# Sinkhorn attention and a gated MLP on one core: the first load from ScalarE, another order of loads, column-wise P, wider transposes of V

## The chip, the cores and the metric

The kernel runs on one core of one Trainium2 chip. The metric is the device time of one execution in microseconds. A core has a TensorE for matrix products (PE in the profile, with its weight loads as PEld), a VectorE (DVE), a ScalarE (ACT), a GpSimd (POOL) and a SyncE (SP), each with a queue of its own, and 16 DMA engines that they share.

## The reference, cut to what matters

```python
P = sort_net                                  # [4, 8, 8, 8]
for _ in range(5):
    P = exp(P - max(P, -1))
    P = P / sum(P, -1)                        # rows
    P = P / sum(P, -2)                        # columns
k_sorted = einsum('bhij,bhjcd->bhicd', P, k_b)    # 8 blocks of 96 tokens
v_sorted = einsum('bhij,bhjcd->bhicd', P, v_b)
attn = softmax(q_b @ k_sorted.T / 8)          # inside each block
x = attn @ v_sorted                           # [4, 768, 512] over the heads
h = relu(x @ w_in); u, v = halves of h
v = layer_norm(v)
out = (u * (w_spatial @ v + b_spatial)) @ w_out
```

4 batches, 8 heads, 768 tokens, 64 per head; q, k, v and all weights are fp32 in memory. The kernel works in bf16 with fp32 accumulation.

## The kernel before, in words

The program is a list of short units in the string `ORDER`, written out by hand. The units are run in the order of the string, and each engine's instructions keep that order in its queue. A unit is a name with arguments: `QT:2:D:0:1` is u_QT with the PSUM tile ps2, the copy on VectorE (D; A is ScalarE), batch 0, pair of heads 1. Batches overlap: while one batch is in the gated MLP, the next is in attention.

**Loads.** `S0` loads sort_net into `p_all` from SyncE's queue. `LH:S:0` loads four heads of the first q as fp32 from SyncE; `QC:A:0` and `QC:A:1` cast it to bf16 on ScalarE (L115). All other loads are `L` units (L171 to L188): GpSimd issues them, and the DMA casts fp32 to bf16. In the string they come as v of batch 0, k of batch 0, the rest of q, then batch 1 and the weights. `IV:2` is a memset of a column of ones in `vm` on GpSimd, `ID` makes the identity on GpSimd, `MA`, `MB` and `MC` derive masks from it.

**Start of ScalarE.** Before any unit ScalarE loads its table of exponentials (L125).

**Sinkhorn.** `SK:0` to `SK:4` are the five rounds on a 32 x 64 tile, one row for each batch and head: exponential on ScalarE (L238), then on VectorE the row sums (L239), their reciprocal, the product with it (L243), the column sums (L244), reciprocal, product (L249). The last round ends in `p_t` (L251). `QC:A:0` stands on ScalarE ahead of the fourth exponential, `QC:A:1` ahead of the fifth.

**From P to the sorted blocks.** `PR:1` spreads P over the partitions by eight small products (L256). `P0` units multiply it by a mask on VectorE (L270) into the block matrices `pd` of batch 0, `PC` copies it out for the later batches, whose `PD` units run on GpSimd. `VT` (L383) multiplies the first batch's v with pd and gives it transposed (`vT`); `KT` does so for k. `VB` (L401) turns vT back block by block: eight transposes, each with a weight load of one block of 96 columns and the 128 columns of the identity moving, then one copy into `vb`. The later batches go another way for v (`VM`, and `VC` by DMA from SyncE). On TensorE stand `PR:1`, one QT, `VT:0`, `KT:3`, `VT:2` in this order.

**Attention.** `SC` makes the scores (L442) and their exponential on ScalarE (L447); `AT` the product with vb (L488), the reciprocal (L495) and the scaling (L496) on VectorE. After it come the transposes `XT`, the products `VP`, `UP`, `SP` and `OP` of the MLP, and the weights' transposes `WW` (L531).

**Idle products.** `DM:ps:n:512` are n products of a zero tile on TensorE with 512 columns (L226), which nobody reads. There are 24 before the first QT and 12 between it and `PR:1`.

**Tiles.** The pool `ld` has eight places for loads, a place is given to the next load once all readers of the old one stand earlier in the order. kT tiles go round six places of `kt_all`, whose last 32 columns are zero, so that a weight load of 128 columns at the last block stays inside; vT tiles are a pool tile with two buffers of 768 columns.

Of the kernel before, what the change touches and what calls it, by code (L numbers as in the profile page):

```python
# [8 lines left out]
FP32 = mybir.dt.float32  # L9
BF16 = mybir.dt.bfloat16  # L10
# [3 lines left out]
AX = mybir.AxisListType  # L14
# [1 line left out]


ORDER = """
S0 CO SK:0 BH LH:S:0 IV:2 L:v:0:0:8 SK:1 SK:2 ID MA L:k:0:0:8 L:q:0:4:8 DM:3:6:512 DM:0:6:512 L:v:1:0:8 L:q:1:0:8
QC:A:0 SK:3 QC:A:1 MB SK:4 DM:2:6:512 DM:1:6:512 MC QT:2:D:0:1 DM:1:6:512 DM:3:6:512 PR:1 L:k:1:0:8 QT:2:A:0:0 P0:0:2  # L20
L:wv L:wsb P0:4:6 P0:6:8 IV:0 P0:2:4 PC:D VT:0:A:0:0 KT:3:D:0:0 L:wu PD:1:0:4 VT:2:A:0:1 L:v:2:0:8 KT:1:A:0:3
KT:0:D:0:2 SC:2:0:0:1 VB:3:D:0:0 PD:1:4:8 KT:1:A:0:1 QT:0:D:0:2 IV:1 QT:2:A:0:3 VB:3:D:0:1 SC:0:0:1:0 VT:1:D:0:3
VT:2:A:0:2 L:wsa L:q:2:0:8 SC:3:0:0:0 PD:3:0:4 PD:3:4:8 BI AT:0:0:0:1 L:k:2:0:8 VB:1:D:0:3 SC:2:0:1:1 AT:3:0:0:0
# [42 lines left out]
def kernel(  # L66
# [25 lines left out]
    HP = H // 2  # L92
# [5 lines left out]
    const = ctx.enter_context(tc.tile_pool(name="const", bufs=1))  # L98
# [6 lines left out]
    def ps_tile(n, dt=FP32):  # L105
        return psum.tile([128, 2, 512 if dt == FP32 else 1024], dt, name=f"ps{n}", tag=f"ps{n}")

    def queue(eng):
        if "general" in st:
            return nc.gpsimd  # L110
        return nc.scalar if eng == "A" else nc.sync
# [10 lines left out]
        else:  # L122
            nc.vector.tensor_scalar_max(out=out, in0=in_, scalar1=0.0)

    nc.scalar.preload_act_table_set("natural_log_exp_and_others")  # L125

    p_all = const.tile([BH, NB, NB], FP32, name="p_all")
    p16 = const.tile([BH, NB * NB], BF16, name="p16")
    p_t = const.tile([BH, NB * NB], BF16, name="p_t")
    spread = const.tile([BH, BH, TB], BF16, name="spread")  # L130
# [20 lines left out]
    NE, NK, NZ, NX = 5, 6, 3, 4  # L151
    ex_all = const.tile([BLK, NE, 2 * NI * BLK + 32], BF16, name="ex_all")
    kt_all = const.tile([128, NK, S + 32], BF16, name="kt_all")
    ex = [ex_all[:, n] for n in range(NE)]
    kt = [kt_all[:, n] for n in range(NK)]

    st = {}
    count = {"e": 0, "k": 0}

    def ld_tile(name):  # L160
        return ld.tile([128, H, G * D], BF16, name=name, tag="ld")
# [31 lines left out]
    def u_S0():  # L193
        load_sort_net()

    def u_BI():
        nc.gpsimd.dma_start(
            out=b_bc, in_=_raw_ap(moe_b_spatial, 0, [[0, 128], [1, S]]))

    def u_CO():  # L200
        nc.vector.memset(warm, 0.0)  # L201
        nc.vector.memset(eps_tile, 1e-6)
        nc.vector.memset(ones, 1.0)
        nc.vector.memset(ex_all[:, :, 2 * NI * BLK:], 0.0)
        nc.vector.memset(kt_all[:, :, S:], 0.0)

    def u_ID():
        make_identity(nc, ident)
# [21 lines left out]
    def u_SK(n, safe=False):  # L230
        n = int(n)
        rows, cols = (first[:, 0:NB], first[:, NB:2 * NB]) if n == 0 else (rowsum, colsum)
        over_rows = lambda x: x.to_broadcast([BH, NB, NB])
        over_cols = lambda x: _raw_ap(x, 0, [x.ap[0], [0, NB], x.ap[1]])
        if safe:
            nc.vector.reduce_max(out=rowsum, in_=p_all, axis=AX.X)
            nc.vector.tensor_sub(out=p_all, in0=p_all, in1=over_rows(rowsum))
        nc.scalar.activation(out=p_all, in_=p_all, func=AF.Exp)  # L238
        nc.vector.reduce_sum(out=rows, in_=p_all, axis=AX.X)  # L239
# [3 lines left out]
        nc.vector.tensor_mul(out=p_all, in0=p_all, in1=over_rows(rowsum))  # L243
        nc.vector.reduce_sum(out=cols, in_=p_all.rearrange("p i j -> p j i"), axis=AX.X)  # L244
# [4 lines left out]
        nc.vector.tensor_mul(out=to, in0=p_all, in1=over_cols(colsum))  # L249
        if n == 4:  # L250
            nc.vector.transpose(out=p_t, in_=p16)  # L251

# [142 lines left out]

    def u_VB(ps, eng, b, hp):
        b, hp = int(b), int(hp)
        t = ps_tile(ps, BF16)[0:BLK, 0, :].rearrange("p (i c) -> p i c", i=NB)
        vT = turned("vT", b, hp)
        for i in range(NB):  # L400
            nc.tensor.transpose(t[:, i, :], vT[:, i * BLK:(i + 1) * BLK], ident)  # L401
        copy(
            eng, vb[b % 2][:, :, 2 * hp:2 * hp + 2, 0:D], t.rearrange("p i (h d) -> p i h d", h=2),
        )

    def u_VM(ps, eng, b, hp):
# [10 lines left out]
            t[:, :, 0:G * D].rearrange("p h (g d) -> p h g d", g=G),  # L417
        )

    def u_VC(b, lo, hi):  # L420
        b = int(b)
        for i in range(int(lo), int(hi)):
            queue("S").dma_start(
                out=vb[b % 2][:, i].rearrange("c h d -> c (h d)"),
                in_=vm[i * TB:(i + 1) * TB].rearrange("t g h d -> t g (h d)"),
            )

    def e_tile(b, hp, ih):
# [398 lines left out]
```

## Time and profile before

| | us |
|---|---|
| median of 3 runs | 156.18 (155.99 to 156.47) |
| span of the profiled execution | 154.5 |
| TensorE busy | 146.7 |
| VectorE busy | 115.4 |
| ScalarE busy | 85.5 |
| GpSimd busy | 39.4 |
| first k: from issue to landing | 11.0 |

The span runs from the first to the last instruction of one execution; the run's own time is longer by what lies around it. Busy times count the idle products as work. In a timeline each row has the start, the length, the engine, the line and operation, the tile written and those read, and in brackets how long the engine sat idle before it and what ended that. Rows named SPq and ACTq are issues of DMAs on those queues. In the rows of the DMA queues stand packets, megabytes and the share of 16 engines' time; q0 is the queue that GpSimd's loads use, q1 that of SyncE and ScalarE.

### The profile page before, as it was taken

To read this page: it belongs to the slowest core of one execution; us is meant where nothing else is said; L and a number is where in the kernel's file an instruction comes from. 1 tells how busy PE (TensorE), PEld (TensorE's weight loads), DVE (VectorE), ACT (ScalarE), POOL (GpSimd) and SP (SyncE) were. 2 spreads that over 40 slices of the span, in tenths; PEclk is the share of its full clock that TensorE was granted. 3 is DMA by queue.
4 is the path that set the end of the run, shared out by engine and by line. 5 is a ranking of instruction groups with operands and counts; after the bars stand their busy time and mean duration, and the time that the engine had idled before them with its cause. 6 is when DMAs were issued, how large, how long until landed. Compare 5 with 4: busy or idle time off the path is not lost.

```text
span 154.5 us, 4033 instructions
## 1 busy us (share of the span) xinstructions
PE 146.7 (95%) x1689; PEld 95.7 (62%) x1689; DVE 115.4 (75%) x258; ACT 85.5 (55%) x116; POOL 39.4 (25%) x45
## 2 busy tenths in 40 slices
PE   6988988999999999999999999999999999999991
PEld 2436866764667777456777654656876556774760
DVE  3787889968899976299974886697977629855742
ACT  3345989787979245997777057357650072260040
POOL 7953663292020007000000044000000406103630
PEclk9999999999999999999999999999999999999999
DMA  2999999999999999990069358704708400307756
GB/s 68 270 204 203 204 206 204 209 216 248 223 205 256 205 231 245 208 195 15 4 118 125 67 102 167 182 3 37 205 0 215 163 0 4 132 4 284 268 191 220
DMA packets 30693, 24.36 MB, mean 158 GB/s; under 512 B 10384, under 2 KB 27792, under 8 KB 30672
## 3 DMA queue, kind: packets, MB, share of 16 engines
q0 software_dynamic: 14432, 12.19, 48.8%
q1 hardware_dynamic: 15664, 11.23, 28.8%
q10 hardware_dynamic: 576, 0.66, 1.2%
q8 instruction: 14, 0.23, 0.6%
q14 instruction: 7, 0.06, 0.1%
HBM read 24.78 MB, written 6.29 MB: 201 GB/s over the span
## 4 chain that ended last, share of the span: by engine, by line
PE 84%; DMA 7%; ACT 2%; DVE 2%; POOL 1%; issue 1%; POOLq 0%; ACTq 0%
PE ps L609 15%; PE ps L554 14%; PE ps L597 14%; PE ps L635 10%; DMA k_in<-in_k_dram 7%; PE ps L442 5%; PE ps L488 5%; PE ps L665 5%; PE ps L383 4%; PE ps L685 3%; PE ps L314 2%; PE ps L410 2%; PE ps L518 2%; ACT ex_all L447 2%; PE ps L531 1%; PE ps L401 1%
## 5 line engine op out<-in xcount | busy, mean ns | idle before, releaser
L626 POOL TENSOR_TENSOR gt<-z,u_sb 128x768 bf16<-128x768 f32 x7 | 11.4, 1640 | 77.0 <-DVE z L615 47.6
L447 ACT ACTIVATE ex_all<-ps 96x768 bf16<-96x768 f32 x32 | 24.7, 806 | 5.7 <-PE ps L442 5.5
L609 PE MATMUL ps<-wspT,v_sb 128*128 128x384 bf16 x144 | 25.1, 326 | 0.0
L597 PE MATMUL ps<-xT,w_in_sb 128*128 128x384 bf16 x128 | 22.8, 326 | 0.0
L496 DVE TENSOR_TENSOR x_sb<-ps,rec_all 96x512 bf16<-96x512 f32 x32 | 22.0, 686 | 1.1
L554 PE MATMUL ps<-w_in_sb,xT 128*128 128x512 bf16 x96 | 22.3, 380 | 0.0
L571 DVE BATCH_NORM_STATS2 stats<-v_sb 128x6 f32<-128x512 bf16 x24 | 16.3, 678 | 4.5 <-ACT v_sb L121 4.5
L115 ACT COPY o_sb<-ps 128x1024 f32<-128x1024 f32 (+1 forms) x12 | 10.9, 905 | 14.6 <-PE ps L685 9.1
L609 PEld LDWEIGHTS <-v_sb 128*128 128x128 bf16 x144 | 13.6, 97 | 8.6
L121 ACT ACTIVATE v_sb<-ps 128x1024 bf16<-128x1024 f32 (+1 forms) x11 | 10.3, 948 | 12.3 <-PE ps L554 12.3
L615 DVE TENSOR_TENSOR z<-ps,b_bc 128x768 f32<-128x768 f32 x12 | 11.4, 954 | 7.3 <-PE ps L609 4.6
L635 PE MATMUL ps<-w_out_sb,gt 128*128 128x256 bf16 x144 | 16.9, 273 | 0.0
L121 ACT ACTIVATE u_sb<-ps 128x768 bf16<-128x768 f32 x12 | 9.7, 811 | 12.7 <-PE ps L597 12.7
L597 PEld LDWEIGHTS <-w_in_sb 128*128 128x128 bf16 x128 | 11.8, 97 | 7.2
L635 PEld LDWEIGHTS <-gt 128*128 128x128 bf16 x144 | 13.8, 97 | 2.1
L554 PEld LDWEIGHTS <-xT 128*128 128x128 bf16 x96 | 8.7, 97 | 9.9
L488 PEld LDWEIGHTS <-ex_all 96*128 96x128 bf16 x256 | 10.7, 97 | 4.0 <-issue 0.5
L488 PE MATMUL ps<-vb,ex_all 96*128 96x65 bf16 x256 | 12.6, 193 | 0.5 <-ACT ex_all L447 0.5
L226 PE MATMUL ps<-warm 128*128 128x512 bf16 x36 | 9.5, 425 | 1.3 <-DVE warm L201 1.3
L442 PE MATMUL ps<-qT,kt_all 64*128 64x96 bf16 x256 | 9.8, 205 | 0.9 <-issue 0.4
L115 ACT CAST kt_all<-ps 128x768 bf16<-128x768 f32 x11 | 8.7, 801 | 2.2 <-PE ps L383 2.2
L442 PEld LDWEIGHTS <-kt_all 64*128 64x128 bf16 x256 | 6.4, 94 | 5.5 <-issue 3.3
(97 smaller groups left out, 202.6 us busy)
## 6 DMA issues: line engine op xcount, KB each, us to landing
out_dram<-o_sb SPq DMA_DIRECT2D x9, 512.0 KB, 4.6
v_in<-in_v_dram POOLq DMA_DIRECT2D x4, 768.0 KB, 21.4
k_in<-in_k_dram POOLq DMA_DIRECT2D x4, 768.0 KB, 23.7
vb<-vm SPq DMA_DIRECT2D x24, 99.0 KB, 5.8
q_in<-in_q_dram POOLq DMA_DIRECT2D x3, 768.0 KB, 28.2
ws_in<-in_moe_w_spatial_dram POOLq DMA_DIRECT2D x2, 576.0 KB, 26.6
w_in_sb<-in_moe_w_in_dram POOLq DMA_DIRECT2D x2, 512.0 KB, 24.9
q<-in_q_dram SPq DMA_DIRECT2D x1, 768.0 KB, 4.6
```

The lines of the kernel that those rows point to most:

```text
L115: nc.scalar.copy(out=out, in_=in_)
L121: nc.scalar.activation(out=out, in_=in_, func=AF.Relu)
L442: nc.tensor.matmul(t[:, hh, 0:HW].rearrange("p (g x) -> p g x", g=G)[:, :, ii * TB:(ii + 1) * TB], lhsT=kT[rows, i * BLK:i * BLK + 128], r ...
L447: nc.scalar.activation(out=e_tile(b, hp, ih).rearrange("p h (x g) -> p h x g", g=G), in_=t[0:BLK, :, 0:HW].rearrange("p h (g x) -> p h x g ...
L488: nc.tensor.matmul(t[:, hh, ii * VW:ii * VW + D + 1], lhsT=e[:, c:c + 128], rhs=vb[b % 2][:, ih * NI + ii, 2 * hp + hh, 0:D + 1], start=Tr ...
L496: nc.vector.tensor_mul(out=x_sb[:, hp].rearrange("p i (h d) -> p h i d", h=2), in0=tv[:, :, :, 0:D], in1=_raw_ap(rec, 0, [rec.ap[0], [NI, ...
L554: nc.tensor.matmul(t[:, x, :], lhsT=st["xT", b][:, n // 3, kc, (n % 3) * 128:(n % 3 + 1) * 128], rhs=w_in_sb[:, kc, DH:DFF], start=(kc == ...
L571: nc.vector.bn_stats(out=stats, in_=st["v_sb", b, n])
L597: nc.tensor.matmul(t[:, x, 0:HW], lhsT=w_in_sb[:, kc, mc * 128:(mc + 1) * 128], rhs=st["xT", b][:, ih, kc, :], start=(kc == 0), stop=(kc = ...
L609: nc.tensor.matmul(t[:, x, 0:HW], lhsT=st["v_sb", b, n][:, mc * 128:(mc + 1) * 128], rhs=wspT[:, 3 * x:3 * x + 3, n, :], start=(n == 0), s ...
L615: nc.vector.tensor_add(out=z.rearrange("p (x c) -> p x c", x=2), in0=t[:, :, 0:HW], in1=b_bc.rearrange("p (x c) -> p x c", x=2),)
L635: nc.tensor.matmul(t[:, x, c:c + w], lhsT=st["gt", b, mc][:, (n0 + x) * 128:(n0 + x + 1) * 128], rhs=w_out_sb[:, mc, c:c + w], start=(mc = ...
```

## The change

Six edits. ScalarE issues the first q, as the first thing that it does, and its table load follows (a new unit `TB`). `L:v:0:0:8` stands directly behind `S0`, ahead of q's issue, and GpSimd's identity comes before the memset `IV:2`. In each Sinkhorn round the row-scaled P goes into a new tile `p_cols` that holds it by columns: the product L243 writes with a stride, the column sum reads contiguously, the product of L249 reads with a stride. The last group of six idle products before `PR:1` has three. vT tiles lie in a new ring `vt_all` of two places with 32 zero columns behind the 768, and the transposes of `VB` load 128 columns as weights, of which the last 32 belong to the next block (or are zero); their results land in partitions 96 to 127, which the copy leaves out. `u_VC` gets arguments that no call uses.

```diff
 ORDER = """
-S0 CO SK:0 BH LH:S:0 IV:2 L:v:0:0:8 SK:1 SK:2 ID MA L:k:0:0:8 L:q:0:4:8 DM:3:6:512 DM:0:6:512 L:v:1:0:8 L:q:1:0:8
-QC:A:0 SK:3 QC:A:1 MB SK:4 DM:2:6:512 DM:1:6:512 MC QT:2:D:0:1 DM:1:6:512 DM:3:6:512 PR:1 L:k:1:0:8 QT:2:A:0:0 P0:0:2
+S0 L:v:0:0:8 LH:A:0 TB CO SK:0 BH ID IV:2 SK:1 SK:2 MA L:k:0:0:8 L:q:0:4:8 DM:3:6:512 DM:0:6:512 L:v:1:0:8 L:q:1:0:8
+QC:A:0 SK:3 QC:A:1 MB SK:4 DM:2:6:512 DM:1:6:512 MC QT:2:D:0:1 DM:1:6:512 DM:3:3:512 PR:1 L:k:1:0:8 QT:2:A:0:0 P0:0:2
...
-    nc.scalar.preload_act_table_set("natural_log_exp_and_others")
-
     p_all = const.tile([BH, NB, NB], FP32, name="p_all")
+    p_cols = const.tile([BH, NB, NB], FP32, name="p_cols")
...
+    vt_all = const.tile([128, 2, S + 32], BF16, name="vt_all")
...
+    def u_TB():
+        nc.scalar.preload_act_table_set("natural_log_exp_and_others")
...
         nc.vector.memset(kt_all[:, :, S:], 0.0)
+        nc.vector.memset(vt_all[:, :, S:], 0.0)
...
-        nc.vector.tensor_mul(out=p_all, in0=p_all, in1=over_rows(rowsum))
-        nc.vector.reduce_sum(out=cols, in_=p_all.rearrange("p i j -> p j i"), axis=AX.X)
+        nc.vector.tensor_mul(out=p_cols.rearrange("p j i -> p i j"), in0=p_all, in1=over_rows(rowsum))
+        nc.vector.reduce_sum(out=cols, in_=p_cols, axis=AX.X)
...
-        nc.vector.tensor_mul(out=to, in0=p_all, in1=over_cols(colsum))
+        nc.vector.tensor_mul(out=to, in0=p_cols.rearrange("p j i -> p i j"), in1=over_cols(colsum))
...
-                st[x, b, hp] = att.tile([128, S], BF16, name=x, tag=x, bufs=2)
+                st[x, b, hp] = vt_all[:, count["v"] % 2]
+                count["v"] += 1
...
-        t = ps_tile(ps, BF16)[0:BLK, 0, :].rearrange("p (i c) -> p i c", i=NB)
+        t = ps_tile(ps, BF16)[:, 0, :].rearrange("p (i c) -> p i c", i=NB)
...
-            nc.tensor.transpose(t[:, i, :], vT[:, i * BLK:(i + 1) * BLK], ident)
+            nc.tensor.transpose(t[:, i, :], vT[:, i * BLK:i * BLK + 128], ident)
         copy(
-            eng, vb[b % 2][:, :, 2 * hp:2 * hp + 2, 0:D], t.rearrange("p i (h d) -> p i h d", h=2),
+            eng, vb[b % 2][:, :, 2 * hp:2 * hp + 2, 0:D], t[0:BLK].rearrange("p i (h d) -> p i h d", h=2),
         )
```

More of the change, by code (lines that the diff above doesn't have):

```diff
@@ L157 @@
     st = {}
-    count = {"e": 0, "k": 0}
+    count = {"e": 0, "k": 0, "v": 0}
     def ld_tile(name):
@@ L418, in u_VM, with u_VC @@
         )
-    def u_VC(b, lo, hi):
-        b = int(b)
+    def u_VC(b, lo, hi, h0=0, h1=HP, eng="S"):
+        b, heads = int(b), slice(2 * int(h0), 2 * int(h1))
         for i in range(int(lo), int(hi)):
-            queue("S").dma_start(
-                out=vb[b % 2][:, i].rearrange("c h d -> c (h d)"),
-                in_=vm[i * TB:(i + 1) * TB].rearrange("t g h d -> t g (h d)"),
+            queue(eng).dma_start(
+                out=vb[b % 2][:, i, heads].rearrange("c h d -> c (h d)"),
+                in_=vm[i * TB:(i + 1) * TB, :, heads].rearrange("t g h d -> t g (h d)"),
             )
```

## The prediction

> **What bounds the kernel now.** I read the page first, then the chain of waits, then the first 16 us and the stretch from 15 to 29 us as a timeline. The page says which engine is scarce, the chain says from when on.
>
> ```profile
> span 154.5 us, 4033 instructions
> PE 146.7 (95%) x1689; PEld 95.7 (62%) x1689; DVE 115.4 (75%) x258; ACT 85.5 (55%) x116; POOL 39.4 (25%) x45
> PE 84%; DMA 7%; ACT 2%; DVE 2%; POOL 1%; issue 1%; POOLq 0%; ACTq 0%
> ```
>
> TensorE is busy 95% of the span, but the 36 idle products at the start count as busy. On the chain 84% is TensorE, and the one large piece that isn't is a transfer at the start. In order of time (start, length in us):
>
> ```profile
> 2.88 10.96 DMA k_in<-in_k_dram
> ...
> 15.99 0.58 PE ps L401 x8
> ...
> 17.69 0.58 PE ps L401 x8
> ...
> 22.12 0.61 PE ps L401 x8
> ...
> 28.75 0.53 PE ps L383 x12
> ```
>
> So the end is set by the landing of the first k at 13.84 us (2.88 + 10.96), then by a mixed stretch in which TensorE, ScalarE and VectorE take turns, and from 28.75 us on by TensorE almost alone. A microsecond taken from the start or from the mixed stretch arrives at the end; the work after 28.75 us isn't touched by the change. So the whole question is how much earlier 28.75 us comes. The start, as a timeline (start, length, engine, line, operation; in brackets the idle time before and who ended it):
>
> ```profile
> 0.75 0.40 SPq L191 DMA_DIRECT2D p_all<-in_sort_net_dram  x1
> 0.82 1.28 ACT L125 ACT_TABLE_LOAD   x1 [0.82 <-PEq L811]
> 1.21 0.42 SPq L348 DMA_DIRECT2D q<-in_q_dram  x1
> 1.29 1.06 POOL L171 DMA_DIRECT2D v_in<-in_v_dram  x1 [0.36 <-issue]
> 2.43 0.26 ACT L238 ACTIVATE p_all<-p_all 32x64 f32<-32x64 f32 x1 [0.32 <-DMA p_all<-in_sort_net_dram]
> 2.88 0.90 POOL L171 DMA_DIRECT2D k_in<-in_k_dram  x1
> 6.12 0.81 ACT L115 CAST q_in<-q 128x768 bf16<-128x768 f32 x1
> 7.71 0.26 ACT L238 ACTIVATE p_all<-p_all 32x64 f32<-32x64 f32 x1 [0.79 <-DVE p_all L249]
> 9.20 2.77 PE L226 MATMUL ps<-warm 128*128 128x512 bf16 x12
> 11.24 0.23 DVE L251 STREAM_TRANSPOSE p_t<-p 32x64 bf16<-32x64 bf16 x1
> 11.41 0.51 DVE L117 COPY qT<-ps 128x768 bf16<-128x768 bf16 x1
> 11.90 0.36 PE L256 MATMUL ps<-p_t,spread 32*128 32x32 bf16 x8
> 12.30 1.41 DVE L270 TENSOR_TENSOR pd<-mask,ps 128x256 bf16<-128x256 bf16 x4 [0.39 <-PE ps L256]
> 12.77 0.53 PE L383 MATMUL ps<-pd,v_in 128*64 128x128 bf16 x12
> 13.89 0.53 PE L383 MATMUL ps<-pd,k_in 128*64 128x128 bf16 x12 [0.59 <-DMA k_in<-in_k_dram]
> 14.79 0.80 ACT L115 CAST vT<-ps 128x768 bf16<-128x768 f32 x1 [0.53 <-PE ps L383]
> ```
>
> Two strands meet at 13.89. The Sinkhorn strand (L238 to L251, then PR at 11.90, P0 at 12.30, the first v product VT at 12.77) is done 0.59 us before k is there. ScalarE's first long wait after it, 0.53 us before 14.79, is for the second VT, which stands behind the k product in TensorE's queue. So the transfer sets the pace and the Sinkhorn strand has about half a microsecond to spare.
>
> **The change part by part.**
>
> *First q from ScalarE, v ahead of the memset: when k lands.* k lands when the DMA engines have moved first q, v and k. What they moved:
>
> ```profile
> 2.00:3.00 1.00, 1.00 (x4) 0.33 (x3) 0.25 (x2) 0.36 (x2) 0.92 (x4) 1.00 0.62 88
> ...
> 4.00:5.00 1.00, 1.00 (x6) 0.39 (x4) 0.61 (x4) 0.26 (x1) 1.00 (x2) 1.00 1.06 398
> ...
> 6.00:7.00 1.00, 1.00 (x7) 0.43 (x5) 0.66 (x4) 0.93 (x2) 1.00 (x2) 1.00 1.30 203
> ```
>
> The last number is GB/s: from 6 us on the engines run at an even 203 GB/s, and between 2 and 5 us they move the first q. Two tensors of 786 KB at 203 GB/s are 7.7 us, and 13.84 - 7.7 is 6.1, which is about where q ends (its issue at 1.21 and 4.6 us to landing, below, give 5.8). The line is full without a gap, so k lands earlier by as much as its front comes earlier. The q issue moves from 1.21, behind p_all's on SyncE, to ScalarE's first free time at 0.82: 0.39 us. The v issue loses the vm memset ahead of it (0.18 us) and starts between 0.75 (when SyncE makes the first issue of all) and 1.1: 0.2 to 0.54 us. The k issue follows ident's two instructions and the moved memset and needs only to be queued by the time v is done. Slow is the stretch from 2 to 3 us (88 GB/s): if what slows it is tied to the clock and not to the issues, only about 0.1 us is won. So 0.1 to 0.5, and I take 0.35: k lands at 13.49, the k product starts at 13.54.
>
> *ScalarE's table load behind that issue.* A DMA issue on ScalarE's queue took
>
> ```profile
> 148.27 0.39 ACTq L697 DMA_DIRECT2D out_dram<-o_sb  x1
> ```
>
> so the table load starts at about 1.25 instead of 0.82 and ends at 2.53; the first exponential starts at about 2.55 to 2.7 instead of 2.43, where it had waited 0.32 us for p_all anyway. I take 0.15 us later for the whole strand. Behind the load wait only the exponentials and q's casts.
>
> *P written by columns.* Per Sinkhorn round, the groups are
>
> ```profile
> L243 DVE TENSOR_TENSOR p_all<-p_all,rowsum 32x64 f32<-32x64 f32 x5 | 1.1, 212 | 0.2
> L244 DVE TENSOR_REDUCE colsum<-p_all 32x8 f32<-32x64 f32 x4 | 1.0, 256 | 0.1
> L249 DVE TENSOR_TENSOR p_all<-p_all,colsum 32x64 f32<-32x64 f32 x4 | 0.8, 212 | 0.1
> L239 DVE TENSOR_REDUCE rowsum<-p_all 32x8 f32<-32x64 f32 x4 | 0.8, 207 | 0.9 <-ACT p_all L238 0.9
> ```
>
> The strided sum costs 49 ns more than the contiguous one of the same shape. The change makes that read contiguous (5 x 0.049 = 0.25 us saved), but the product of L243 now writes with the stride and that of L249 reads with it. Neither shows in the trace. If neither costs anything: -0.25 us; if each costs the 49 ns: +0.25. The read is nearest to the strided sum and probably costs the same, the write I put at half: +0.1 us.
>
> *Three idle products less.* PR at 11.90 stood behind twelve of them that end at 11.97 while p_t was ready at 11.47. Three are 3 x 2.77 / 12 = 0.69 us. With ScalarE's strand 0.15 later and the rounds 0.1 longer p_t is ready at about 11.72, PR runs at 11.75 instead of 11.90, VT at about 12.64 and it ends at 13.2, before k at 13.5. So on the path the three products are worth nothing; they pay for what the table load and the stride may cost. If that cover were gone (nine products kept at twelve), VT would end at about 13.6 and cost 0.1 us.
>
> *V transposes by 128-column weights.* Four groups of eight (VB, L401). Their weight load and the nearest transposes with full weights and the same 128 moving columns:
>
> ```profile
> L401 PEld LDWEIGHTS <-vT 128*96 128x96 bf16 x32 | 2.1, 123 | 0.5 <-issue 0.3
> L531 PEld LDWEIGHTS <-ws_in 128*128 128x128 bf16 x36 | 2.2, 97 | 0.5 <-issue 0.2
> ...
> 47.18 0.67 PE ps L531 x12
> ...
> 16.00:18.00 2.00, 2.00 (x51) 1.83 (x52) 1.67 (x3) 1.93 (x4) 1.98 (x4) 1.00 1.33 210
> ```
>
> On the chain eight of L401 take 0.58 us, and of L531 twelve take 0.67, so eight 0.45: 0.13 us a group at most. Three groups lie on the chain (15.99, 17.69, 22.12). All four kept: 0.5 us. But the last row, of 16 to 18 us, has ScalarE busy for 1.93 of 2 us and VectorE for 1.67 (the fourth and third of the columns with counts; TensorE has 2.00): what TensorE saves ahead of their work may be waited for again; none kept: 0. I take 0.2 us.
>
> The extra memset of vt_all and the moved identity lie in VectorE's and GpSimd's first 3 us, while VectorE waits for the first exponential. The ring vt_all has two places as the old tile had. u_VC's new arguments keep their defaults.
>
> **Sum.** 0.35 (k's landing) + 0.2 (V transposes) = 0.55 us off the span: 154.5 - 0.55 = 153.95. The median of the runs lies 1.68 us over this span (156.18 - 154.5); with that, 155.6 us.
>
> **The rivals.**
>
> *A: only the V transposes count.* k lands as before because the slow stretch of 2 to 3 us stays where it is, or the Sinkhorn strand becomes the later one. For it speaks that the strand has only 0.59 us to spare and takes 0.15 to 0.5 us of cost before the 0.4 us that the idle products give back. Then 0 to 0.3 us is won: 156.0.
>
> *B: both gains come through whole.* k 0.5 earlier and the transposes 0.4: 155.3. For it speaks that TensorE, not ScalarE, leads the chain from 15.64 to 20.5; against it ScalarE's full queue. This lies in the same direction as the forecast and I count it with it.
>
> *C, slower: v gets in ahead of q in the DMA engines.* Now the two are issued within 0.08 us of each other, q first, and the trace shows what followed. From 3 to 5 us only the hardware queue moved data, though v's issue had ended at 2.35; from 34 to 39 us both queues moved at once:
>
> ```profile
> q<-in_q_dram SPq DMA_DIRECT2D x1, 768.0 KB, 4.6
> ...
> q1 hardware_dynamic: 403, 0.62, 84.1%
> ...
> q0 software_dynamic: 716, 0.57, 71.8%
> q1 hardware_dynamic: 706, 0.65, 48.6%
> ```
>
> So what comes first is served first at the start, and two queues with a backlog share. After the change v may be issued at 0.75 and q at 0.82. If v comes first, its 786 KB take 3.9 us from about 2 us, and then q shares with k at 0.65 MB per 5 us, 6 us more, or goes at its own pace (403 packets, 0.62 MB in 2 us), 2.5 us: q lands between 8.4 and 11.9, say 10.1 instead of 5.8. The cast of q at 6.12 stands on ScalarE ahead of the fourth exponential (7.71), so that one would start at 10.1 + 0.81 = 10.9, 3.2 us late. All of the Sinkhorn strand behind it, PR, P0 and VT move by that, 0.8 us of it is covered (ScalarE's wait of 0.53 before 14.79, and some 0.3 of the time in which PR stood behind idle products), and 0.2 comes back from the transposes: +2.2 us, 158.4. It decides once q lands after about 7.9 us, since up to there the 0.8 us of cover and the transposes pay. Against it: the relation of the two issues hardly changes, and q's data flowed in the window from 2 to 3 us, within 1.8 us of its issue, while v's hadn't come by 5, 3.7 us after its own. The Trainium skill, DMA: Bandwidth & Descriptors, section Queues, rings and completion order, says that each engine takes turns between the queues that have work; by that rule q and v would share from the start whenever both are there, q at 0.65 MB per 5 us would land at about 8, and the result would be about no change, 156.2. The rows from 34 to 39 us agree with it, those from 3 to 5 us don't show it; I count this milder form with C's chance and with the middle.
>
> **How the numbers follow.** The forecast with B 0.60, A 0.25, C 0.12 (a third of it the milder form), something else 0.03. A measurement of this kernel tells a difference from none at about 0.3%, 0.47 us: faster means under 155.71, slower over 156.65. The forecast's own range is 155.1 to 156.0, so some of its chance, 0.10, falls within; A falls within, but for a tenth. Faster 0.52, the same 0.36, slower 0.12. The range for 8 in 10 takes in the whole of the forecast and of A: 155.0 at the lower end (0.5 + 0.5 and some) to 156.4.
>
> **What would show it.** Right: the wait of the first k product still ends by the DMA, at 13.3 to 13.7; the first exponential at 2.55 to 2.7; PR within 0.3 of 11.75; L401's weight loads at 97 ns; L244 at 207, L249 near 256, L243 between 212 and 256. The stretch from the k product to the first product of L383 at 28.75 shorter by 0.1 to 0.3. Wrong: the k product waits for pd (VectorE, L270) and not for the DMA; the cast of q starts later than 7.9; or k lands at 13.8 again. What the sum stands on most weakly is that the full line of transfers starts earlier when its issues do.

## The result and the profile after

| | before | after |
|---|---|---|
| median of 7 runs, us | 156.18 (155.99 to 156.47) | 155.51 (155.04 to 158.08) |
| ratio after / before, 95% interval | | 0.9962 (0.9948 to 0.9977) |
| span of the profiled execution, us | 154.5 | 153.8 |

One execution of the changed kernel, at 158.08 us and a lower granted clock, is left out of the ratio. The change makes the kernel 0.4% faster (0.3% in a second measurement, below), and 155.51 lies beside the 155.6 that was forecast. That the two lie so near is partly luck: as the experiments show, more than half of the gain between the two profiles came by other terms than those in the sum.

The page of the changed kernel: the span, the engines, and the shares of the chain that ended last.

```profile
span 153.8 us, 4021 instructions
PE 146.5 (95%) x1679; PEld 95.6 (62%) x1686; DVE 115.7 (75%) x259; ACT 85.4 (56%) x116; POOL 39.3 (26%) x45
PE 85%; DMA 7%; ACT 2%; DVE 2%; issue 1%; POOL 1%; POOLq 0%; ACTq 0%
```

At this level the two pages can't be told apart: 0.7 us is too little to move a share. The chain of the changed kernel in order of time shows where it lies (start, length; lines from L353 on have moved down by 5, so L388 is the old L383, L406 the old L401, L670 the old L665):

```profile
2.96 10.67 DMA k_in<-in_k_dram
...
13.68 0.88 PE ps L388 x24
...
15.78 0.55 PE ps L406 x8
...
17.46 0.55 PE ps L406 x8
...
19.08 0.23 PE ps L447 x5
19.31 0.20 issue
19.51 0.25 PE ps L447 x3
...
21.72 0.61 PE ps L406 x8
...
28.36 0.53 PE ps L388 x12
...
137.53 7.80 PE ps L670 x48
```

The same places in the chain of the kernel before, as far as they were not shown:

```profile
19.34 0.15 PE ps L442 x2
19.48 0.37 issue
19.85 0.30 PE ps L442 x6
...
138.09 7.80 PE ps L665 x48
```

Three stretches give the 0.56 us by which the last products of the MLP start earlier (138.09 to 137.53), and a fourth the rest of the 0.73 us between the two spans (154.53 and 153.80):

- The first k product starts 0.21 us earlier (13.89 to 13.68). That is k's landing.
- From it to the next batch's k product pass 14.68 instead of 14.86 us: 0.18. Two groups of V transposes take 0.55 instead of 0.58, the third 0.61 as before, so 0.06 for the wider weights. Most of the rest is a stall of TensorE inside the third group of scores, put down to "issue": 0.20 instead of 0.37, and from 19.08 (19.34) to the next operation, at 19.76 (20.16), pass 0.68 instead of 0.82 us.
- From there to L670 pass 109.17 instead of 109.34 us: 0.17, in a stretch that was taken to be untouched.
- From L670 to the end of the span pass 16.27 instead of 16.44 us: another 0.17 there.

The start of the changed kernel as a timeline (start, length, engine, line and operation, in brackets the idle time before and who ended it):

```profile
0.82 0.45 ACTq L353 DMA_DIRECT2D q<-in_q_dram  x1
1.25 1.06 POOL L171 DMA_DIRECT2D v_in<-in_v_dram  x1 [0.80 <-POOLq L816]
1.31 1.28 ACT L197 ACT_TABLE_LOAD   x1 [1.31 <-PEq L816]
2.60 0.26 ACT L242 ACTIVATE p_all<-p_all 32x64 f32<-32x64 f32 x1
6.38 0.81 ACT L115 CAST q_in<-q 128x768 bf16<-128x768 f32 x1
11.63 0.23 DVE L255 STREAM_TRANSPOSE p_t<-p 32x64 bf16<-32x64 bf16 x1
12.01 0.35 PE L260 MATMUL ps<-p_t,spread 32*128 32x32 bf16 x8 [0.39 <-DVE p_t L255]
12.87 0.53 PE L388 MATMUL ps<-pd,v_in 128*64 128x128 bf16 x12
13.68 0.53 PE L388 MATMUL ps<-pd,k_in 128*64 128x128 bf16 x12 [0.28 <-DMA k_in<-in_k_dram]
```

q's issue sits at 0.82 and v's has hardly moved (1.29 to 1.25): GpSimd's first issue waits 0.80 us with nothing ahead of it. The Sinkhorn strand is later (first exponential +0.17, p_t +0.39, first v product +0.10), and the k product still waits for the DMA. The groups by line:

```profile
L247 DVE TENSOR_TENSOR p_cols<-p_all,rowsum 32x64 f32<-32x64 f32 x5 | 1.3, 261 | 0.2
L253 DVE TENSOR_TENSOR p_all<-p_cols,colsum 32x64 f32<-32x64 f32 x4 | 1.0, 255 | 0.1
L248 DVE TENSOR_REDUCE colsum<-p_cols 32x8 f32<-32x64 f32 x4 | 0.8, 207 | 0.1
L406 PEld LDWEIGHTS <-vt_all 128*128 128x128 bf16 x32 | 1.9, 97 | 0.5 <-issue 0.3
```

The column sum has lost its 49 ns, the strided write has cost 49 and the strided read 43, and the weight loads of the V transposes have gone from 123 to 97 ns.

### The profile page after: what moved, and what is told of

The parts are those of the page before. It is cut to its first block, busy times and chain, and to the rows that moved or that the text cites. A ratio compares the mean times of both kernels' runs of the same rounds, so it can differ in the third digit from the quotient of the medians.

```text
span 153.8 us, 4021 instructions
## 1 busy us (share of the span) xinstructions
PE 146.5 (95%) x1679; PEld 95.6 (62%) x1686; DVE 115.7 (75%) x259; ACT 85.4 (56%) x116; POOL 39.3 (26%) x45
## 3 DMA queue, kind: packets, MB, share of 16 engines
q1 hardware_dynamic: 15136, 10.44, 26.4%
q10 hardware_dynamic: 1104, 1.44, 2.8%
## 4 chain that ended last, share of the span: by engine, by line
PE 85%; DMA 7%; ACT 2%; DVE 2%; issue 1%; POOL 1%; POOLq 0%; ACTq 0%
PE ps L614 15%; PE ps L559 14%; PE ps L602 14%; PE ps L640 10%; DMA k_in<-in_k_dram 7%; PE ps L493 5%; PE ps L447 5%; PE ps L670 5%; PE ps L388 4%; PE ps L690 3%; PE ps L319 2%; PE ps L415 2%; PE ps L523 2%; ACT ex_all L452 2%; PE ps L536 1%
## 5 line engine op out<-in xcount | busy, mean ns | idle before, releaser
L631 POOL TENSOR_TENSOR gt<-z,u_sb 128x768 bf16<-128x768 f32 x7 | 11.4, 1642 | 76.7 <-DVE z L620 47.4
L620 DVE TENSOR_TENSOR z<-ps,b_bc 128x768 f32<-128x768 f32 x12 | 11.4, 954 | 6.9 <-PE ps L614 5.1
L640 PEld LDWEIGHTS <-gt 128*128 128x128 bf16 x144 | 13.8, 98 | 2.0
```

The costliest lines, as they stand in the source:

```text
L620: nc.vector.tensor_add(out=z.rearrange("p (x c) -> p x c", x=2), in0=t[:, :, 0:HW], in1=b_bc.rearrange("p (x c) -> p x c", x=2),)
L640: nc.tensor.matmul(t[:, x, c:c + w], lhsT=st["gt", b, mc][:, (n0 + x) * 128:(n0 + x + 1) * 128], rhs=w_out_sb[:, mc, c:c + w], start=(mc = ...
```

## The experiments

### Which part brings it

**The loads alone.** Before, with only the new order of loads:

```diff
-S0 CO SK:0 BH LH:S:0 IV:2 L:v:0:0:8 SK:1 SK:2 ID MA
+S0 L:v:0:0:8 LH:A:0 TB CO SK:0 BH ID IV:2 SK:1 SK:2 MA
```

> The kernel before with the new order of loads alone: q from ScalarE ahead of the table load, v ahead of the memset, the identity earlier; P by rows, twelve idle products, 96-column transposes. Theory: k lands at 13.6 as in the changed kernel, the first exponential at 2.6, the spreading of P at 12.15 behind the idle products, k's product at 13.7; the next batch's k product at about 28.55, ratio 0.998. Rival (the loads need the other edits): k's product no earlier than 13.85 and ratio 0.9995 to 1.001.

Measured: 155.96 us (155.62 to 158.48, 12 runs), ratio 1.0004 (0.9985 to 1.0024). The k product starts at 13.28 in the profile. That is the ratio that the rival gave, though k's product came earlier than either expected. Nine executions lie at 155.62 to 156.08, five of them below all 30 of the kernel before in the same session (155.84 and more); three lie at 157.05, 157.11 and 158.48. So the loads seem to bring some tenths in part of the executions and to lose them in late ones, which the kernel before doesn't have; a gain over all executions isn't shown.

**The V transposes alone.** Before, with the ring `vt_all`, its memset, and the 128-column weights:

```diff
+    vt_all = const.tile([128, 2, S + 32], BF16, name="vt_all")
-                st[x, b, hp] = att.tile([128, S], BF16, name=x, tag=x, bufs=2)
+                st[x, b, hp] = vt_all[:, count["v"] % 2]
-            nc.tensor.transpose(t[:, i, :], vT[:, i * BLK:(i + 1) * BLK], ident)
+            nc.tensor.transpose(t[:, i, :], vT[:, i * BLK:i * BLK + 128], ident)
```

> The kernel before with the 128-column V transposes alone. Theory (they give 0.2 us whatever the start is): k's product at 13.85 to 13.9 as before, weight loads of 97 ns, the next batch's first k product at 28.55 instead of 28.75, ratio 0.9985 to 0.999, and executions as close together as those of before (0.6 us). Rival (ScalarE's queue takes it back): 28.75 and ratio 1.000.

Measured: 155.65 us (155.50 to 155.94, 11 runs), ratio 0.9977 (0.9967 to 0.9987). This part alone brings 0.38 us, more than expected, though the chain of the changed kernel shows 0.06 us for the wider weights. So something else in it works.

**The changed kernel with 96-column transposes**, the ring kept:

```diff
-            nc.tensor.transpose(t[:, i, :], vT[:, i * BLK:i * BLK + 128], ident)
+            nc.tensor.transpose(t[:, i, :], vT[:, i * BLK:(i + 1) * BLK], ident)
```

> The changed kernel with its V transposes back at 96-column weights, all else kept. Theory (k's landing gave 0.2 us, the wide transposes 0.2 us by the first late k product): the first k product stays at 13.7 us, the weight loads of the V transposes take 123 ns, and the first k product of the next batch comes at 28.55 instead of 28.36; the time lies at 0.997 to 0.998 of before. Rival (the transposes were hidden and all of the 0.4 us is the start): that product stays at 28.36 and the time at 0.996.

Measured: 155.96 us (155.13 to 157.90, 12 runs), ratio 0.9996 (0.9968 to 1.0023), again with three late executions (157.11, 157.45, 157.90); the other nine have a median of 155.59, beside 155.51 of the changed kernel. The weight loads take 123 ns again. A ratio of 0.997 to 0.998 was expected; the interval takes that in, and no gain at all as well. By itself this was inconclusive, since late executions and the width could not be told apart; so the ring was tried alone.

**The ring alone.** Before, with `vt_all` and its memset, and the transposes as they were:

```diff
+    vt_all = const.tile([128, 2, S + 32], BF16, name="vt_all")
-                st[x, b, hp] = att.tile([128, S], BF16, name=x, tag=x, bufs=2)
+                st[x, b, hp] = vt_all[:, count["v"] % 2]
+        nc.vector.memset(vt_all[:, :, S:], 0.0)
```

> The kernel before with vT in the new ring (and its memset), but the V transposes still with 96-column weights: it differs from the run of the wide transposes alone by nothing but those weights. In the traces so far a group of eight V transposes takes 0.54 to 0.56 us from its start to the next group's with either width, so the theory now is that the width gives about 0.05 us and what the run of the wide transposes gained (ratio 0.9977) lies elsewhere: then this kernel also comes to 0.997 to 0.9985. Rival (the width gives it): ratio 0.9995 to 1.0005. TensorE stalls on its instructions at about 19.3 us in either case.

Measured: 155.66 us (155.47 to 155.82, 10 runs), ratio 0.9976 (0.9967 to 0.9986), the same as with the wide weights. So the width gives nothing that can be measured, and the gain belongs to what comes with the ring: one memset more in VectorE's queue and other places in SBUF. In the two traces all engines have the same instructions otherwise. Two places account for 0.34 of the 0.37 us (0.24% of 155.97). The first lies at 100 to 103 us; VectorE's rows and the weight loads of two groups of scores, first before, then the ring alone:

```profile
100.05 0.96 DVE L615 TENSOR_TENSOR z<-ps,b_bc 128x768 f32<-128x768 f32 x1 [0.87 <-PE ps L488]
101.94 0.69 DVE L496 TENSOR_TENSOR x_sb<-ps,rec_all 96x512 bf16<-96x512 f32 x1
102.34 0.53 PEld L442 LDWEIGHTS <-kt_all 64*128 64x128 bf16 x16 [0.32 <-issue]
```

```profile
99.36 0.96 DVE L618 TENSOR_TENSOR z<-ps,b_bc 128x768 f32<-128x768 f32 x1 [0.50 <-PE ps L612]
101.26 0.69 DVE L499 TENSOR_TENSOR x_sb<-ps,rec_all 96x512 bf16<-96x512 f32 x1
102.02 0.37 PEld L445 LDWEIGHTS <-kt_all 64*128 64x128 bf16 x16 [0.32 <-issue]
```

The sixteen loads end 0.16 us sooner with the ring, but no load is faster: each takes 91 to 95 ns in both. Before, the ninth, with which the second group begins, starts 0.23 us behind the eighth (102.45 and 102.68). It waits for VectorE, whose scaling L496 ends at 102.63; with the ring that scaling ends at 101.95, and nothing waits. VectorE lost the time at the sum z (L615, with the ring L618): before, the wait for TensorE is over at 99.63 and z starts at 100.05, 0.41 us later, with nothing in the trace that it still waits for. In the loads alone, the other kernel without the ring, it is also 0.41 us, and in all twelve kernels with it 0.04 or 0.05. From about 99 us to L670 pass 38.28 us before and 38.29 with the loads alone, and 38.11 to 38.13 in the kernels with the ring in which this was read; that is the 0.17 us of the third stretch above. Why VectorE stands still at z is open. Its queue has one instruction more ahead of z with the ring, and an 8-KB packet of instructions starts at 100.75 and 99.96 us in the two kernels without the ring and at 90.5 to 95.1 in the others, so the blocks in which its instructions come are one candidate; no run tried the memset without the ring.

The second place is the end. From the last products (L670) to the end of the span pass 16.44 and 16.45 us in the two kernels without the ring and 16.26 to 16.28 in eleven of the twelve with it (16.71 with P in two halves, below). Here the wait for the last store ends 1.98 us behind its issue before and 1.83 with the ring alone; why is open too.

### What lies hidden

**P by rows again**, in the changed kernel:

```diff
-        nc.vector.tensor_mul(out=p_cols.rearrange("p j i -> p i j"), in0=p_all, in1=over_rows(rowsum))
-        nc.vector.reduce_sum(out=cols, in_=p_cols, axis=AX.X)
+        nc.vector.tensor_mul(out=p_all, in0=p_all, in1=over_rows(rowsum))
+        nc.vector.reduce_sum(out=cols, in_=p_all.rearrange("p i j -> p j i"), axis=AX.X)
```

> The changed kernel with P kept by rows in one tile, as before (strided column sum, no strided write). Theory (the column-wise tile costs 43 to 49 ns on each of two products and saves 49 on the sum, and the Sinkhorn strand isn't the one that k's product waits for): the transpose of P moves from 11.63 to about 11.4 us, the first v product from 12.87 to about 12.6 us, k's product stays at 13.7 and the time within 0.1% of the changed kernel. Rival (the strand sets the pace by ScalarE's copies): the second v product's copy and all behind it come 0.15 us earlier.

Measured: 155.38 us (155.10 to 155.71, 7 runs), ratio 0.9961 (0.9948 to 0.9975). The groups by line of this run:

```profile
L247 DVE TENSOR_TENSOR p_all<-p_all,rowsum 32x64 f32<-32x64 f32 x5 | 1.1, 212 | 0.2
L248 DVE TENSOR_REDUCE colsum<-p_all 32x8 f32<-32x64 f32 x4 | 1.0, 254 | 0.1
L253 DVE TENSOR_TENSOR p_all<-p_all,colsum 32x64 f32<-32x64 f32 x4 | 0.8, 212 | 0.1
```

The columns cost 5 x (49 + 43 - 47) = 0.22 us net, and undoing them moves the time by less than the interval: they lie beside the transfer of k. (P's transpose came at 11.53 us and not at the 11.4 expected, because P itself landed late in this execution and the first exponential started at 2.73 instead of 2.60.)

**Six idle products again** instead of three (`DM:3:3:512` to `DM:3:6:512`):

```diff
-DM:1:6:512 DM:3:3:512 PR:1
+DM:1:6:512 DM:3:6:512 PR:1
```

> The changed kernel with six idle products ahead of the spreading of P, as before, instead of three. Theory (they are cover for a strand that became 0.39 us later): the spreading of P moves from 12.01 to about 12.3, the first v product to about 13.15 and its end to 13.7, so k's product stays within 0.1 us of 13.68, but the second v copy on ScalarE, at 14.59, moves by about 0.1; the time within 0.1% of the changed kernel. Rival (the three products are the gain): all from 13.68 on comes 0.3 us later and the ratio to before is 0.998 or more.

Measured: 155.77 us (155.23 to 157.82, 12 runs), ratio 0.9980 (0.9964 to 0.9997). TensorE's timeline in this run:

```profile
9.55 2.76 PE L230 MATMUL ps<-warm 128*128 128x512 bf16 x12
12.24 0.36 PE L260 MATMUL ps<-p_t,spread 32*128 32x32 bf16 x8
...
13.12 0.53 PE L388 MATMUL ps<-pd,v_in 128*64 128x128 bf16 x12
13.45 0.53 PE L388 MATMUL ps<-pd,k_in 128*64 128x128 bf16 x12
```

PR stands 0.23 us later, and the k product follows the v product without a wait: k had landed at 13.21 in this execution, so here the three products cost some 0.2 us (an estimate, from the 0.23 of PR). In the profiled execution of the changed kernel, with k at 13.64, they would have cost nothing. The ratio is the rival's 0.998, but the interval takes in the changed kernel's second ratio, 0.9973, and this profile loses another 0.2 us at 96.9 us, where TensorE waits for a transfer of vb.

### When k lands, and where q may be issued

When the first and the last of the 16 DMA engines had done their share of the first k, read from the trace's semaphore events:

```
q issued by        kernel                 first    last (us)
SyncE,  1.21       before                 13.08    13.84
SyncE,  1.22       V transposes alone     12.97    13.48
SyncE,  1.22       ring alone             12.98    13.42
SyncE,  1.22       q from SyncE again     13.08    13.45
ScalarE, 0.82      changed                12.77    13.64
ScalarE, 0.83      changed, second time   12.67    13.24
ScalarE, 0.83      loads alone            12.66    13.14
ScalarE, 0.83      narrow transposes      12.65    13.77
ScalarE, 0.83      P by rows              12.75    13.32
ScalarE, 0.83      six idle products      12.71    13.21
```

The first engine is done 0.2 to 0.4 us earlier when ScalarE issues q. The last engine's lag, 0.37 to 1.12 us in this list, is as large as the gain and differs between executions, and k is there only when the last one is done. So the last ones overlap: 13.42 to 13.84 us with q from SyncE, 13.14 to 13.77 from ScalarE, with the middle of each list (13.47 and 13.28) 0.2 us apart.

**q from SyncE again**, the table load first:

```diff
-S0 L:v:0:0:8 LH:A:0 TB CO SK:0
+TB S0 LH:S:0 L:v:0:0:8 CO SK:0
```

> The changed kernel with the table load first again and q issued by SyncE behind the small load of P; v stays the first load, and all other edits stay. Theory (what moves k's landing is q's issue, and what spreads the executions of the kernels with the new loads over up to 2.5 us is that q may now get ahead of P's 8 KB): the first exponential at 2.43, k lands at 13.8, the ratio 0.998 to 0.9985 and no execution over 156.5 us. Rival 1 (v ahead of q spreads them): executions at 157 and above remain. Rival 2 (v's issue moved k's landing): k lands at 13.6 and the ratio is 0.996.

Measured: 155.63 us (155.33 to 155.93, 11 runs), ratio 0.9977 (0.9968 to 0.9986).

```profile
1.22 0.42 SPq L353 DMA_DIRECT2D q<-in_q_dram  x1
...
2.53 0.26 ACT L242 ACTIVATE p_all<-p_all 32x64 f32<-32x64 f32 x1 [0.42 <-DMA p_all<-in_sort_net_dram]
...
13.49 0.53 PE L388 MATMUL ps<-pd,k_in 128*64 128x128 bf16 x12 [0.18 <-DMA k_in<-in_k_dram]
```

k's product starts at 13.49, though k was expected to land at 13.8 with q's issue back at 1.22: the landing in one execution doesn't tell the two issues apart. By the ratios q's issue by ScalarE is worth 0.04 to 0.15% (0.9977 against 0.9973 and 0.9962), 0.06 to 0.23 us, which the intervals don't tell from nothing.

**The changed kernel a second time**, as it is, for the spread:

> The changed kernel once more, for the spread of its executions. Theory (in some executions P's small load falls behind q's in the DMA engines, since the two are now issued 0.07 us apart on two queues): most executions at 155.0 to 156.0 us, one to three of eleven at 157 to 158.5, and none between 156.5 and 157 for any other cause; the profile, if it falls on a late one, has the first exponential waiting for P's load up to 4 or 5 us. Rival (the late executions of the earlier variants came from their own edits): none over 156.5.

Measured: 155.34 us (155.16 to 156.49, 12 runs), ratio 0.9973 (0.9956 to 0.9990). The result stands. None of the twelve is over 156.5 us, as the rival said and not as was expected; but the 158.08 of the first measurement is this kernel's too, so late executions don't come from the variants' own edits alone. Put together, the kernels in which ScalarE issues q beside SyncE's load of P (the changed one twice, the loads alone, narrow transposes, P by rows, six idle products) were over 156.5 us in 9 of 62 executions, up to 158.48. With q behind P on SyncE none was: 89 executions of the kernel before stay under 156.48, 37 of four others (three above, and the last one below) under 155.95. Only 16 of these 37 have v as the first load, so that v alone makes executions late is unlikely but not excluded: at 9 in 62, chance would leave 16 without a late one about one time in ten. ScalarE's loads go by a queue of their own: when the first q moves to ScalarE, q1 falls from 11.23 to 10.44 MB and q10 rises from 0.66 to 1.44, so q1 is SyncE's and not, as said ahead, that of both. P and q, on one queue before, are on two after the change. In the trace P's first packet starts at 1.77 us and q's at 1.96: 0.19 us apart. The three runs that follow ask what an inversion costs.

**P's load behind q's**, both from ScalarE:

```diff
-S0 L:v:0:0:8 LH:A:0 TB
+L:v:0:0:8 LH:A:0 S0 TB
-        load_sort_net()
+        nc.scalar.dma_start(out=p_all, in_=sort_net.rearrange("b h i j -> (b h) i j"))
```

> The changed kernel with P's load issued by ScalarE behind q's, so that its packets surely stand behind q's in each DMA engine. Theory (first come, first served): P lands only when q has, at about 5 us instead of 2.4; the first exponential starts at about 5.2 and the whole Sinkhorn strand 2.6 us later, the first v product at 15.4; less some 0.7 us of cover, the time is 2 us over the changed kernel, near 157.5, where the late executions lie. Rival (the engines take turns between the two): P lands at 3.0 to 3.5 us, the exponential behind the table load at 3.1 to 3.6, and the time 0.3 to 0.6 us over the changed kernel.

Measured: 158.53 us (158.00 to 160.07, 6 runs), ratio 1.0130 (1.0115 to 1.0146). ScalarE's timeline:

```profile
5.62 0.26 ACT L242 ACTIVATE p_all<-p_all 32x64 f32<-32x64 f32 x1 [2.48 <-DMA p_all<-in_sort_net_dram]
```

P's 8 KB wait for all 786 KB of q, which lands at 5.43, P itself at 5.60, and the Sinkhorn strand becomes the bound.

**P in two halves**, both from SyncE, so that only the second half, issued at about 1.15 us, falls behind q's issue, on a queue of its own:

```diff
-        queue("S").dma_start(out=p_all, in_=sort_net.rearrange("b h i j -> (b h) i j"))
+        for lo in (0, BH // 2):
+            queue("S").dma_start(
+                out=p_all[lo:lo + BH // 2], in_=sort_net.rearrange("b h i j -> (b h) i j")[lo:lo + BH // 2])
```

> The changed kernel with P's load in two halves on SyncE, so that the second half is issued at about 1.15 us on its own queue, 0.3 us behind q's issue on ScalarE instead of 0.07 ahead of it. Theory (first come, first served in each engine, whatever the queue): the second half lands only when q does, at about 5 us, the first exponential starts at about 5.2 to 5.6 and the time is 158 to 159. Rival (queues take turns, and P behind q on ScalarE's own queue was late only by the order of one queue): the first exponential at 2.6 to 3.2 us and the time within 0.6 us of the changed kernel.

Measured: 159.13 us (158.99 to 159.58, 4 runs), ratio 1.0206 (1.0189 to 1.0223). ScalarE's timeline, and the busy time of each engine by stretches of 4 us (sum and count for TensorE, its loads, VectorE, ScalarE, GpSimd, then the granted clock, the DMA share and GB/s):

```profile
5.33 0.26 ACT L244 ACTIVATE p_all<-p_all 32x64 f32<-32x64 f32 x1 [2.74 <-DMA p_all<-in_sort_net_dram]
```

```profile
8.00:12.00 4.00, 1.23 (x13) 0.50 (x13) 3.27 (x15) 1.95 (x4) 1.77 (x4) 1.00 1.31 204
12.00:16.00 4.00, 4.00 (x33) 1.58 (x29) 2.55 (x13) 0.76 (x2) 0.00 (x0) 0.62 1.31 203
```

Another queue didn't help: 4 KB issued 0.3 us behind q landed at 5.24 us, 0.2 ahead of q. The late strand leaves TensorE idle for 2.8 of 4 us, and the granted clock falls to 0.62 in the next stretch, so the products behind it run slowly as well. The latest executions above, 157.82 to 158.48 us, lie at or just below the lower end of the times of these two kernels, 158.00 to 160.07, and the mean clock of the four latest (0.985 to 0.989) is that of the second of these kernels (0.986 to 0.989). In the other traces the last share of P lands at 2.27 to 2.51 us, but at 2.61 with six idle products and at 2.70 with P by rows, two kernels in which ScalarE issues q. That an inversion of P and q, or part of one, makes the late executions is argued from this: no late execution was caught in a trace.

**q issued behind the first exponential**, so that v comes first for certain:

```diff
-S0 L:v:0:0:8 LH:A:0 TB CO SK:0
+S0 L:v:0:0:8 TB CO SK:0 LH:A:0
```

> The changed kernel with q's issue on ScalarE behind the first exponential, so that v comes first in the DMA engines. By the slow rival of the prediction (v first, then q shares with k or follows v): q lands between 8.4 and 11.9 us, its cast starts then instead of at 6.38, the fourth exponential is 2 to 4 us late and the time is 157.5 to 159.5. Rival (the engines take turns from the start): q lands at about 8, ratio to before 1.000 to 1.004. How early v's data flow shows how long its issue takes when nothing stands before it.

Measured: 160.75 us (159.83 to 161.00, 4 runs), ratio 1.0309 (1.0292 to 1.0325). ScalarE's timeline, then the DMA queues from 5.5 to 10.5 us (q10 is the queue of q here, q0 that of v):

```profile
2.31 0.43 ACTq L353 DMA_DIRECT2D q<-in_q_dram  x1
...
11.07 0.83 ACT L115 CAST q_in<-q 128x768 bf16<-128x768 f32 x1 [4.91 <-DMA q<-in_q_dram]
```

```profile
q0 software_dynamic: 723, 0.54, 69.6%
q10 hardware_dynamic: 523, 0.78, 49.9%
```

v's first packet starts at 3.04 us, 1.78 behind its issue at 1.26, and q's, issued at 2.31, only at 5.38; then the two share, and q lands at 11.05. This is the order of rival C, with q issued 1.5 us later than C has it, and the price is higher than worked out.

### A version meant to beat both

The changed kernel with q from SyncE as above, P by rows, and the first k in two loads, so that the first two blocks land earlier:

```diff
-S0 L:v:0:0:8 LH:A:0 TB CO SK:0 BH ID IV:2 SK:1 SK:2 MA L:k:0:0:8
+TB S0 LH:S:0 L:v:0:0:8 CO SK:0 BH ID IV:2 SK:1 SK:2 MA L:k:0:0:2 L:k:0:2:8
```

> A version meant to beat both: the changed kernel with the table load first and q from SyncE behind P, P by rows, and the first k in two loads, heads 0 and 1 ahead of the rest. Theory (k's landing is the last wait of the start and the Sinkhorn strand the next): k's first product no longer waits for the DMA and starts at 12.9 to 13.0, right behind the first v product; the second v copy on ScalarE starts at about 14.0 instead of 14.6; ratio to before 0.992 to 0.995, and no execution over 156.5. Rival (the next k product, which needs all of k, or ScalarE's copies take the place of the wait): ratio 0.996 to 0.998.

Measured: 155.11 us (155.06 to 155.52, 5 runs), ratio 0.9949 (0.9936 to 0.9961): faster than the kernel before; against the changed kernel (0.9962 and 0.9973) the intervals overlap. Its timeline:

```profile
12.49 0.53 PE L388 MATMUL ps<-pd,v_in 128*64 128x128 bf16 x12
...
12.82 0.53 PE L388 MATMUL ps<-pd,k_in 128*64 128x128 bf16 x12
...
27.85 0.53 PE L388 MATMUL ps<-pd,k_in 128*64 128x128 bf16 x12 [0.60 <-DMA k_in<-in_k_dram]
```

The first k product now stands right behind the v product, 0.86 us earlier than in the changed kernel, but only 0.51 of it arrives at the next batch's k product (28.36 to 27.85): that one now waits 0.60 us for its own load. The limit has moved to the next transfer on the full line.

## Why the prediction was right, and where not

**What bounds the kernel** was read rightly for the start. The 0.21 us by which the k product starts earlier in the two profiles are still there at the next batch's k product, and when the Sinkhorn strand is made late (P behind q, q behind v) it sets the time instead. The step "the work after 28.75 us isn't touched by the change" failed: 0.34 of the 0.73 us between the profiles lie behind that point.

**k's landing, 0.35.** The mechanism is right for the front, which comes earlier by what was said (first engine 12.97 to 13.08 with q from SyncE, 12.65 to 12.77 from ScalarE), and in the profile k lands inside the range of 0.1 to 0.5, at 0.2. Mis-sized is the step "k lands earlier by as much as its front comes earlier": k's time is that of the slowest of 16 engines, and in the time of the kernel the loads alone brought nothing that can be told from none (1.0004). And the step "the v issue ... starts between 0.75 and 1.1" failed, it started at 1.25, since what held it back was not the memset. q's part of the term was the whole of it.

**Table load, +0.15:** +0.17, hidden, as said.

**P by columns, +0.1:** +0.22 on the strand. The step that was mis-sized is the write "put at half": it costs 49 ns, as much as the strided sum had lost. The Trainium skill, SBUF — State Buffer, section Door 1: The DMA port swizzle, says that each access that crosses to a new 16-byte line pays a penalty, and that fp32 may stride over 4 elements for free; the stride here is 8 elements, and the trace agrees for the write and the read alike.

**Idle products, nothing on the path:** right for the profiled execution (PR at 12.01 instead of 11.75, and TensorE still waits 0.28 us for k). With k at 13.2, as in others, the three products taken out are worth some 0.2 us by the estimate above; the cover was smaller than the 0.59 us of one profile.

**V transposes, 0.2:** wrong in its reason. The loads fell from 123 to 97 ns as forecast, but the step "of L531 twelve take 0.67, so eight 0.45" failed: a group of eight takes 0.55 (0.58 before), so a group's time doesn't scale with its count. The Trainium skill, TensorE: Matmul & The Clock Gate, section Weight-path perf modes, says that the fast weight load is on at 128 weights of a type other than fp32; the load's duration agrees, and the ring alone shows that the kernel's time doesn't follow.

**What took its place.** The edit of the V transposes measured 0.38 us, 0.34 of it by what the ring brought along: the wait for VectorE at 102 us and the end of the last store. Both lie behind 28.75 us, in work that was dismissed because no instruction in it had changed, though VectorE's queue and the places of tiles had. That this makes up for the terms that came out smaller, and puts 155.51 beside 155.6, is luck.

Some 0.14 come from the stall at 19 us. Its rows stood in the profile of before and were not read. In the trace a 16-KB packet of the instruction queue starts at 17.54 us before and 17.25 after, and the products resume 2.3 us later in both (19.85, 19.51); the stall falls after the second of eight products before and after the fifth in the changed kernel, and with three idle products less there are just three pairs of load and product less ahead of that point. So it is probably TensorE's next block of instructions that is waited for. The packet starts 3.2 to 3.8 us behind the first k product in all fourteen traces, and also where k had landed early and the product came late (P behind q: 13.14, 17.47, packet at 20.75), so it comes earlier as the products do. The same arithmetic holds with the V transposes alone (17.36, 19.58, a stall of 0.50); with the loads alone the packet starts at 16.76, and the products, due there at about 19.1, don't stall. With the ring alone it starts at 17.21, the products are due at 19.5, and the stall that was expected at 19.3 doesn't come. That the packet is TensorE's own block is inferred from this arithmetic; no run tried it by itself. The packet's own transfer takes 0.95 us of the 2.3; the rest is not explained. The Trainium skill, Runtime: NRT & Kernel Launch, section Instruction fetch mechanics, says that blocks of 16 KiB are fetched ahead and that this is mostly hidden; the size agrees, and here, if the inference holds, 0.2 and 0.37 us were not hidden.

**The rivals.** A said that only the V transposes count and k would not land earlier. In the profiles k did, by 0.2; but as to which edit brings the time A is nearer to the experiments than the forecast is, since the edit of the V transposes alone brought 0.38 us and the loads alone nothing that can be told from none. B's direction was right, its sizes not. C did not happen, and not narrowly: q's data came at 1.96 us and v's could not come before 3.04, so the margin is a microsecond, not the "0.08 us of each other" of the issues. Its price, 158.4, looks too low: q landed at 11.05 instead of the 10.1 taken, 1 us more, part of which may be its later issue in that run, and the clock fell (0.976 to 0.989 as a mean). The milder form, by the rule that engines take turns between queues (the Trainium skill, DMA: Bandwidth & Descriptors, Queues, rings and completion order), is seen from 5.5 to 10.5 us in that run, where both have a backlog; at the start the 4 KB behind q contradict it, which landed only 0.2 us ahead of q. The slower case that the late executions point to was one not listed: P, not v, in a race with q.

## What to carry to other kernels

When a transfer that sprays over many engines sets the pace, its end is the slowest engine's, so look at several executions before a few tenths of a microsecond are promised to an earlier issue, and don't let a large load race a small one that everything waits for. Cost a shorter instruction by the change of its whole group in a row of the same count, not by a rate. When an edit adds a tile, undo the tile apart from what it is for: here what came along with it, one instruction more and other places, was worth more than its purpose. And when a group of instructions takes longer, see whether each one does or one of them waits.

## What the runs showed of the hardware beyond that

- TensorE stood still with nothing to wait for at about 19.3 us, for 0.04 to 0.50 us in seven of the traces, and resumed 2.2 to 2.4 us behind the start of a 16-KB packet of instructions; VectorE stood still for 0.41 us at z in the two kernels without the ring.
- GpSimd's first issue of a load starts at 1.25 us with nothing ahead of it, and its data 1.78 us later where q comes behind it (4.63 us in the changed kernel, behind q); ScalarE's at 0.82, its data 1.1 us later.
- When the idle products go from a pace of 0.42 to 0.21 us differs between executions: at 4.15 us before, 5.90 in the changed kernel, 7.15 with the ring alone, where 24 of them took 8.19 us and PR came at 12.56. A mean over one profile of the warm-up is no constant.
